# Last powers in bf16, paired table copies, a shorter gate mask and a new written order: a gated attention and state-space mix on one NeuronCore

## The chip, the cores and the metric

The kernel runs on 1 core of a Trainium2 chip. The metric is the device time of one execution in microseconds (us). The program is one launch; nothing is computed on the host. Five engines work side by side: PE (matrix products; its weight loads are shown apart as PEld), ACT (scalar engine), DVE (vector engine), POOL, and SP, which here issues every DMA.

## The reference

An input `x` of 2048 tokens by 512 channels goes through two branches that are mixed by a gate for each token.

```
g = sigmoid((x * gate_w).sum(-1))                 # one gate for each token
a = A(x)        # 32 heads of 16 channels, 4 segments of 512 tokens:
                # causal softmax attention inside a segment, plus a linear
                # memory of the earlier segments (M, z), mixed by sigmoid(beta)
b = B(x)        # diagonal state-space model, 512 channels x 128 states:
                # K[d,l] = Re sum_n C[d,n] dB[d,n] exp(dt A[d,n] l)
                # y = causal convolution of x with K (by FFT), + x * Dskip
out = g * a + (1 - g) * b
```

The positions `l` of the convolution are rounded to bf16 in the reference, so only some of the 2048 exponents differ.

## The kernel before

**Attention.** For each segment `s` and each group `hg` of 8 heads the kernel projects keys and queries (`project`, tags `pk`, `pq`; `ko` is a masked copy of the keys), makes the values (`seg_tokens`, tags `tok`), five score tiles of 128x2048 with an exponential on ACT (`scores`, tags `sc`, L1067), a causal mask product on DVE from the second half of the segments on (`mk`, L1079), products with the values (`pv`), a division (`nrm`, L1041 and L1042), the memory part (`mem`, with feature maps `fq`), a transpose (`oT`), and at the end the output projection (`fin`). There are 80 score tiles; their exponentials are the largest work of ACT.

**Convolution kernel.** `ssm_prep` computes the complex step factor Z for two halves `h` of the channels. `ssm_powers` squares it again and again: power k is Z to 2^k, kept in f32 (a square on ACT, L785; a subtraction and a product on DVE, L786 and L787), copied to bf16 (tag `pwc`, L793 on ACT or L794 on DVE), with a negated half (L795) and a 64 KB DMA that puts the real part in a second place. `tables(c)` then makes, for each of four chunks `c` of 128 channels, two tables F (20 entries) and G (32 entries) of products of powers: four copies of powers into F and one copy of the coefficients into G (tag `tabc`, by the helper `evac`, L226 on ACT or L227 on DVE), twelve complex products of three DVE instructions each (tags `tab<c>.<n>`, L1180, L1183, L1187), then 8 groups of small matrix products (tag `lag<c>`, PE, 128x40) whose results are evacuated by ACT or DVE and sent by DMA into `KTT`.

**Convolution.** `x_level1` transforms x and writes it to a DRAM scratch (`xl1`). `tail(half)` runs 16 steps `t` for each half: it loads constants (`CT`, 192 KB, and `CD`, 320 KB, both c_DNM) and x (`Zx`), makes X and the transformed kernel K on PE, exchanges the halves of X by two 64 KB DMAs, multiplies on DVE (`Y`, L1298), transforms back (`V`), and writes. `fir` and `Cl` finish and bring the result into the token layout for `fin`. K of half a needs lag0 and lag1, K of half b needs lag2 and lag3.

**Order.** The text `ORDER` sets everything: each entry is the number of an operation, with `a` (ACT) or `v` (DVE) where either engine can run it, and the buffer slots that it takes. An engine runs its operations strictly in that order; SP issues its DMAs strictly in that order. `S.replay` reads the text and `S.emit` writes the waits. On one engine the tags stand thus in the order before:

```
DVE  ... tab1.11 tab1.11 nrm0.3.1 pk1.1 sm0.1 ...
SP   ld_prm0 ld_ident ld_prm0 ld_dt xTl0 xl1l0 ld_W1 ld_prm1 ld_small
     ld_prm1 ld_wq0 ld_prm2 ld_negm ld_wk0 ld_mk ld_small ld_prm2 ld_wv ...
SP   ... Xb15 Xb15 CDb2 Xb3 Xa15 CTb5 Xa15 Xb3 CDb3 CTb1 Zxb6 CDb4 ...
```

**Gates.** `gates` makes the mask `gmaskT` (544 columns, f32) in two steps: L865 copies 512 gate values into it, L866 multiplies all 544 columns by the block mask `bdT`.

Of the kernel before, what the change touches and what calls it, by code (L numbers as in the profile page):

```python
# [7 lines left out]
ACT = mybir.ActivationFunctionType  # L8
# [501 lines left out]
def build_graph(nc, es, A_x, A_wq, A_wk, A_wv, A_wo, A_beta, B_A_re, B_A_im, B_B_re, B_B_im,  # L510
# [264 lines left out]
    def ssm_powers(Zs):  # L775
        Zc = list(Zs)
        for k in range(10):
            for h in range(2):
                S.tag = "pow%d.%d" % (h, k)
                Z = Zc[h]  # L780
                pw = Tile(pwP, BF16)
                pws[(k, h)] = pw
                if k < 9:
                    sq, nz = Tile(sqPs[h], F32), Tile(ZPs[h], F32)
# [676 lines left out]
```

## Time and profile before

| | |
|---|---|
| median of 3 runs | 287.18 us (286.94 to 287.20) |
| the profiled execution | 287.07 us, its span 285.3 us |
| PE busy | 248.9 us (87%) |
| DVE busy | 265.6 us (93%), 634 instructions |
| ACT busy | 261.4 us (92%), 314 instructions |
| POOL busy | 5.9 us |
| granted clock of PE | 0.994 on average |

The span runs from the first to the last instruction; 1.8 us of the execution's own time lie around it. A line of a group gives the busy time, the mean duration of one instruction, and the idle time of its engine just before. Durations on DVE and ACT overlap: the next instruction starts before the one ahead has ended, so what a piece of work costs its engine is the distance from start to start. Times in the timeline are from the start of the span.

### The profile page before, as it was taken

What the parts mean: (1) busy time and instruction counts of PE and PEld (TensorE: products, weight loads), DVE (VectorE), ACT (ScalarE), POOL (GpSimd) and SP (SyncE); (2) the same over time, 40 slices, a digit from 0 to 9 for tenths busy, and PEclk for the clock granted to TensorE, in tenths of its full rate; (3) what the DMA queues carried; (4) which work ended last, traced back from release to release, by engine and by line L of the source; (5) the groups of instructions that cost most, each with busy time, mean ns of one, the idle gap of its engine ahead of it and who ended that gap; (6) DMA issues with size and microseconds to landing.
All of it is one profiled execution on the core that took longest, in us unless ns stands there. A gap on an engine that the chain in (4) does not pass through costs nothing.

```text
span 285.3 us, 9041 instructions
## 1 busy us (share of the span) xinstructions
PE 248.9 (87%) x3741; PEld 170.4 (60%) x3776; DVE 265.6 (93%) x634; ACT 261.4 (92%) x314; POOL 5.9 (2%) x9
## 2 busy tenths in 40 slices
PE   2767778788687999999999899999989999999995
PEld 1423444465344756777767477876766676889552
DVE  1999999999999999999999999996889999999795
ACT  2999999999999999989999999999878999998832
POOL 0003100000001000000001000000000000000000
PEclk9999997999999999999999999999999999999999
DMA  6969364402825727653656576787667876356966
GB/s 179 212 209 169 97 155 149 149 7 84 122 88 169 181 58 208 186 165 87 177 174 194 137 219 181 194 242 200 192 199 210 258 209 190 77 146 175 264 175 203
DMA packets 61211, 47.71 MB, mean 167 GB/s; under 512 B 23921, under 2 KB 57074, under 8 KB 61170
## 3 DMA queue, kind: packets, MB, share of 16 engines
q1 hardware_dynamic: 61170, 47.13, 60.1%
q8 instruction: 30, 0.49, 0.8%
q14 instruction: 11, 0.09, 0.1%
HBM read 26.79 MB, written 8.39 MB: 123 GB/s over the span
## 4 chain that ended last, share of the span: by engine, by line
PE 35%; DVE 33%; ACT 26%; issue 2%; DMA 2%; SPq 0%; DVEq 0%
PE psum L663 34%; ACT sb L1067 16%; ACT sb L226 8%; DVE sb L1180 5%; DVE sb L1187 5%; DVE sb L1183 5%; DVE sb L227 3%; DVE sb L794 2%; DVE sb L787 2%; DVE sb L786 2%; DMA sb<-sb 1%; DVE sb L1042 1%; DMA sb<-in_B_A_im_dram 1%; ACT sb L940 1%; DVE sb L795 1%
## 5 line engine op out<-in xcount | busy, mean ns | idle before, releaser
L663 PE MATMUL psum<-sb 128*128 128x17 bf16 (+12 forms) x3605 | 241.3, 231 | 26.8 <-ACT sb L1067 14.3
L663 PEld LDWEIGHTS psum<-sb 128*128 128x128 bf16 (+4 forms) x3640 | 161.3, 99 | 100.9 <-ACT sb L1067 27.5
L1067 ACT ACTIVATE sb<-psum 128x2048 bf16<-128x2048 f32 x80 | 152.1, 1901 | 4.7 <-PE psum L663 3.8
L226 ACT ACTIVATE sb<-psum 128x512 bf16<-128x512 f32 (+4 forms) x154 | 88.4, 628 | 3.2 <-PE psum L663 2.8
L1180 DVE TENSOR_TENSOR sb<-sb 128x512 bf16<-128x512 bf16 (+3 forms) x48 | 33.0, 697 | 0.0
L1187 DVE TENSOR_TENSOR sb<-sb 128x512 bf16<-128x512 bf16 (+3 forms) x48 | 32.1, 681 | 0.0
L1183 DVE TENSOR_TENSOR sb<-sb 128x512 bf16<-128x512 bf16 (+3 forms) x48 | 31.9, 674 | 0.0
L227 DVE CAST sb<-psum 128x512 bf16<-128x512 f32 (+2 forms) x41 | 27.6, 674 | 3.0 <-PE psum L663 2.8
L1079 DVE TENSOR_TENSOR sb<-sb 128x1024 bf16<-128x1024 bf16 (+1 forms) x40 | 22.4, 569 | 1.3 <-ACT sb L1067 1.2
L1298 DVE TENSOR_TENSOR sb<-sb 128x1024 bf16<-128x1024 bf16 x32 | 21.7, 680 | 1.9 <-DMA sb<-sb 1.8
L1042 DVE TENSOR_TENSOR sb<-psum,sb 128x256 bf16<-128x256 f32 x32 | 13.2, 414 | 0.1
L227 DVE COPY sb<-psum 128x512 bf16<-128x512 bf16 (+2 forms) x15 | 7.2, 480 | 5.7 <-PE psum L730 5.3
L785 ACT ACTIVATE sb<-sb 128x512 f32<-128x512 f32 x18 | 11.8, 656 | 0.0
L1368 ACT ACTIVATE sb<-psum,sb 128x512 bf16<-128x512 f32 x8 | 5.2, 689 | 5.7 <-DMA out_dram<-sb 5.5
L1041 DVE RECIPROCAL sb<-psum 128x16 f32<-128x16 f32 x32 | 7.9, 248 | 1.4 <-PE psum L663 1.3
L912 POOL COPY sb<-sb 128x128 bf16<-128x128 bf16 x4 | 5.5, 1462 | 149.1 <-PE psum L663 124.0
L1121 DVE TENSOR_TENSOR sb<-psum,sb 128x512 bf16<-128x512 f32 x12 | 8.2, 684 | 0.1
L794 DVE CAST sb<-sb 128x512 bf16<-128x512 f32 x19 | 8.0, 434 | 0.0
L996 ACT ACTIVATE sb<-sb 128x512 bf16<-128x512 bf16 x12 | 7.5, 636 | 0.1
L940 ACT ACTIVATE sb<-psum 128x512 bf16<-128x512 bf16 x12 | 7.6, 637 | 0.0
L1337 DVE TENSOR_TENSOR sb<-psum,sb 128x512 bf16<-128x512 f32 x11 | 7.4, 687 | 0.2 <-PE psum L663 0.2
L786 DVE TENSOR_TENSOR sb<-sb 128x256 f32<-128x256 f32 x18 | 7.5, 417 | 0.0
(74 smaller groups left out, 120.7 us busy)
## 6 DMA issues: line engine op xcount, KB each, us to landing
sb<-c_DNM SPq DMA_DIRECT2D x28, 320.0 KB, 3.8
sb<-sb SPq DMA_DIRECT2D x84, 64.0 KB, 2.9
sb<-c_DNM SPq DMA_DIRECT2D x28, 192.0 KB, 3.1
scr_Z<-sb SPq DMA_DIRECT2D x16, 256.0 KB, 2.2
sb<-scr_Z SPq DMA_DIRECT2D x32, 128.0 KB, 3.1
sb<-sb SPq DMA_DIRECT2D x32, 128.0 KB
sb<-in_A_x_dram SPq DMA_DIRECT2D x5, 512.0 KB, 4.8
scr_C<-sb SPq DMA_DIRECT2D x8, 256.0 KB, 2.6
```

The lines of the kernel that those rows point to most:

```text
L226: fa = lambda e: e.activation(dst(), src(), ACT.Copy)
L227: fd = lambda e: e.tensor_copy(dst(), src())
L663: mm = lambda e, o_, l, r_, st, sp, **kw: e.matmul(o_, lhsT=l, rhs=r_, start=st, stop=sp, skip_group_check=True, **kw)
L786: op("DVE", ("V1", 256), lambda e, nz=nz, sq=sq: e.tensor_tensor(ap(nz, 0, n=256), ap(sq, 0, n=256), ap(sq, 256, n=256), ALU.subtract), r= ...
L794: "DVE": (("Vs2", 512), lambda e, dst=dst, src=src: e.tensor_copy(dst(), src()))})
L1042: op("DVE", ("V1", 256), lambda e: e.tensor_tensor(ap(o1, gi * 16, [[128, 4], [32, 4], [1, 16]]), ap(T, dims=[[68, 4], [17, 4], [1, 16]]), ...
L1067: o = op("ACT", ("Ax", 2048), lambda e, P=P, pT=pT: e.activation(ap(pT, n=2048), ap(P, n=2048), ACT.Exp, scale=0.25), r=[P], w=[pT])
L1079: op("DVE", ("V2", 128 * nb), lambda e, pT=pT, dims=dims: e.tensor_tensor(ap(pT, dims=dims + [[1, 128]]), ap(pT, dims=dims + [[1, 128]]), ...
L1180: op("DVE", ("V2" if n > 1 else "V1", 256 * n), lambda e: e.tensor_tensor(run(tile, ne, dst, 1), run(tile, ne, src, sstep), fac(cl * 512), ...
L1183: op("DVE", ("V2" if n > 1 else "V1", 256 * n), lambda e: e.tensor_tensor(run(t2, n, 0, 1), run(tile, ne, src, sstep), fac(cl * 512 + 256) ...
L1187: op("DVE", ("V2" if n > 1 else "V1", 256 * n), lambda e: e.tensor_tensor(D_(), D_(), ap(t2, n * 128, [[-n * 128, 2], [2 * n, 64], [1, 2 * ...
L1298: op("DVE", ("V2", 1024), lambda e, Y=Y, XAB=XAB, K3=K3: e.tensor_tensor(ap(Y, dims=[[512, 2], [1, 512]]), ap(XAB, dims=[[512, 2], [1, 512 ...
```

## The change

1. **Powers** (`ssm_powers`). At k = 8 the square of power 8 is written straight into the bf16 tile of power 9 (subtraction and product with bf16 outputs). The f32 tile for it and its copy are gone, once for each half: two copies fewer.
2. **Tables** (`tables`). Four copies of 256 columns into F become two of 512 columns: entries 2 and 3 (powers 1 and 2), entries 4 and 11 (powers 3 and 0). Eight copies fewer in all; the copy into G stays.
3. **Gate mask** (`gates`). The 512 gate values are multiplied by the block mask on their way into `gmaskT`; the other 32 columns get a product of their own.
4. **Order.** A new text `ORDER`. Operations from power 9 on have new numbers.

```diff
@@ ssm_powers
                 if k < 9:
+                    pws[(k, h)] = Tile(pwP, BF16)
+                pw = pws[(k, h)]
+                if k == 8:
+                    last = Tile(pwP, BF16)
+                    pws[(9, h)] = last
+                    sq = Tile(sqPs[h], F32)
+                    half = lambda T, o: ap(T, o, [[128, 2], [1, 128]])
+                    op("ACT", ("As", 512), ... ACT.Square ...)
+                    op("DVE", ("V1", 256), ... e.tensor_tensor(ap(last, 0, [[512, 2], [1, 128]]), half(sq, 0), half(sq, 256), ALU.subtract) ...)
+                    op("DVE", ("V1", 256), ... e.scalar_tensor_tensor(ap(last, 256, [[512, 2], [1, 128]]), half(Z, 0), 2.0, half(Z, 256), ALU.mult, ALU.mult) ...)
+                elif k < 9:
...
-                op("ANY", 0, None, r=[Z], pw=[pw], ... copy to bf16, ACT or DVE ...)
+                if k < 9:
+                    op("ANY", 0, None, r=[Z], pw=[pw], ... copy to bf16, ACT or DVE ...)
@@ gates
-        op("DVE", ("V1", 512), lambda e: e.tensor_copy(ap(gmaskT, dims=[[17, 32], [1, 16]]), ap(growT, dims=[[1, 32], [0, 16]])), r=[growT], w=[gmaskT])
-        op("DVE", ("V1", 544), lambda e: e.tensor_tensor(ap(gmaskT, dims=[[136, 4], [1, 136]]), ... ap(bdT, dims=[[0, 4], [1, 136]]), ALU.mult), r=[bdT], w=[gmaskT])
+        op("DVE", ("V1", 32), lambda e: e.tensor_tensor(ap(gmaskT, 16, [[136, 4], [17, 8]]), ... ap(bdT, 16, [[0, 4], [17, 8]]), ALU.mult), r=[bdT], w=[gmaskT])
+        op("DVE", ("V1", 512), lambda e: e.tensor_tensor(ap(gmaskT, 0, [[136, 4], [17, 8], [1, 16]]), ap(bdT, 0, [[0, 4], [17, 8], [1, 16]]),
+                                                         ap(growT, 0, [[8, 4], [1, 8], [0, 16]]), ALU.mult), r=[bdT, growT], pw=[gmaskT])
@@ tables
-        for e_, k_ in ((11, 0), (2, 1), (3, 2), (4, 3)):
-            S.evac(lambda e_=e_: ap(F, 2 * e_, [[FPL, 2], [2 * NF, 64], [1, 2]]),
-                   lambda k_=k_: ap(pws[(k_, h)], cl * 512, [[256, 2], [2, 64], [1, 2]]), 256, ...)
+        for e0, e1, ka, kb in ((2, 3, 1, 2), (4, 11, 3, 0)):
+            def src2(ka=ka, kb=kb):
+                a_ = ap(pws[(ka, h)], cl * 512, n=1)
+                return ap(pws[(ka, h)], cl * 512, [[ap(pws[(kb, h)], cl * 512, n=1).offset - a_.offset, 2], [256, 2], [1, 128]])
+            S.evac(lambda e0=e0, e1=e1: ap(F, 2 * e0, [[2 * (e1 - e0), 2], [2 * NF, 128], [1, 2]]), src2, 512, ...)
@@ ORDER (two entries as an example: xT0, then CTb5)
-59a
+59v
-1583/4
+1573/2
```

What the new order changes, read from the text by tags:

- Evacuations that change engine ahead of the lag products of chunk 3: from ACT to DVE one of `xT0` (1024 columns), `pwc1.8`, one of `lag1`, `tok2.0` and `Va9`; from DVE to ACT one of `oT0`. Of the table copies, two of chunk 1 and one of chunk 3 were on ACT; now all eight paired copies are on DVE, and the G copy of chunk 1 is on ACT. Later ones go both ways: 11 from DVE to ACT and 11 from ACT to DVE among X, K and V of the convolution, and a few of `lag3`, `fir`, `oT`, `pk`, `pq` and `gts`.
- DVE ahead of the last product of chunk 3: `diag` (128 columns) and one `fq1.3` newly stand before it, one `sm1.0` no longer does. Ahead of the last product of chunk 0 newly stand three products of the second half's powers 2 and 3; at the end of chunk 1 they stand before it in both orders.
- PE: the operations ahead of each chunk's lag products are the same set in both orders, except one `pv1.0` that moves behind lag1. At the start PE now runs `xl1 xl1 xl1 pk0.0 xl1 prm1 pq0.0 tok0.3 prm2 sc0.0` instead of `xl1 xl1 xl1 prm1 pq0.0 pk0.0 prm2 tok0.1 sc0.0`.
- SP at the start: `ld_prm0 ld_ident ld_prm0 ld_dt xTl0 ld_small ld_W1 xl1l0 ld_wk0 ld_wq0 ld_prm1 ld_wv ld_mk ld_prm1 ld_prm2 ld_negm ld_prm2 ...`: the value weights (`ld_wv`, 512 KB) stand ahead of the second half of the B coefficients (`ld_prm1`) and of both loads of the C coefficients (`ld_prm2`).
- SP at step 5 of half b: `... Xb15 Xb15 Xa15 CTb5 Zxb1 CDb2 Xa15 CDb4 CTb1 Xb3 CDb3 Xb2 ...`: the constants of step 5 (`CTb5`) now go ahead of `CDb2` and of the exchange of step 3.

More of the change, by code (lines that the diff above doesn't have):

```diff
@@ L440 @@
+951/1/1/0 912 952 1770/0/2 934 927/1 953 944/0/3 954 945 1728 1760/2/3 935 931 1742/3/4 913/4 1729 946 1732/5/5 1771 932 914v 1772 1507/0 1761 936
+1765 1773 939/0 1762 943 947 937/0 1766 948 1743 1744 1739/4/2 1767/2/3 1745 1731 1746/3/1 949/4 1737 938/1 950 1733 955 1740 1738 1778/6/4 956/1
+1753/0/0 1734 957a 1741 1779 1768 1780 1769 1774/1/5 1747 1756/2/2 1775 1757 1754 1787/7/3 1788 1748 1781 1755 1776 1749/6/1 1783/4/0 1758 1789 1782
+1790 1777 1759 1791 1750 1751 1752 1784 1785 1786
 """
@@ L780, in ssm_powers @@
                 Z = Zc[h]
-                pw = Tile(pwP, BF16)
-                pws[(k, h)] = pw
                 if k < 9:
+                    pws[(k, h)] = Tile(pwP, BF16)
[5 more added lines that the diff above has]
+                    half = lambda T, o: ap(T, o, [[128, 2], [1, 128]])
+                    op("ACT", ("As", 512), lambda e, sq=sq, Z=Z: e.activation(ap(sq, n=512), ap(Z, n=512), ACT.Square), r=[Z], w=[sq], key=PW[h] + PWS * k)
+                    op("DVE", ("V1", 256), lambda e, last=last, sq=sq, half=half: e.tensor_tensor(ap(last, 0, [[512, 2], [1, 128]]), half(sq, 0), half(sq, 256), ALU.subtract),
+                       r=[sq], pw=[last], key=PW[h] + PWS * k)
+                    op("DVE", ("V1", 256), lambda e, last=last, Z=Z, half=half: e.scalar_tensor_tensor(ap(last, 256, [[512, 2], [1, 128]]), half(Z, 0), 2.0, half(Z, 256), ALU.mult, ALU.mult),
+                       r=[Z], pw=[last], key=PW[h] + PWS * k)
+                elif k < 9:
                     sq, nz = Tile(sqPs[h], F32), Tile(ZPs[h], F32)
@@ L791, in ssm_powers @@
                 dst = lambda pw=pw: ap(pw, 0, [[512, 2], [256, 2], [1, 128]])
-                op("ANY", 0, None, r=[Z], pw=[pw], key=PW[h] + PWS * k + 0.3, alts={
-                    "ACT": (("As", 512), lambda e, dst=dst, src=src: e.activation(dst(), src(), ACT.Copy)),
-                    "DVE": (("Vs2", 512), lambda e, dst=dst, src=src: e.tensor_copy(dst(), src()))})
+                if k < 9:
+                    op("ANY", 0, None, r=[Z], pw=[pw], key=PW[h] + PWS * k + 0.3, alts={
+                        "ACT": (("As", 512), lambda e, dst=dst, src=src: e.activation(dst(), src(), ACT.Copy)),
+                        "DVE": (("Vs2", 512), lambda e, dst=dst, src=src: e.tensor_copy(dst(), src()))})
                 op("DVE", ("V4", 256), lambda e, pw=pw: e.tensor_scalar(
```

144 lines of the change are left out of this document (70 added, 74 removed).

## Prediction

> **What bounds the kernel now.** I read three views: the busy time of the engines by stage, the chain of waits where a stage ends, and the timeline of DVE there. I cut the stages where the lag products of chunks 1, 2 and 3 start, at about 92.4, 128.0 and 165.3 us.
>
> ```profile
> core 0: us, PE busy (x) PEld busy (x) DVE busy (x) ACT busy (x) POOL busy (x), PEclk, DMA share, GB/s
> 6.40:92.40 86.00, 65.54 (x903) 37.56 (x915) 85.82 (x214) 84.90 (x113) 4.73 (x3) 0.98 0.55 135
> 92.40:128.00 35.60, 33.52 (x575) 24.36 (x580) 35.49 (x85) 33.73 (x43) 0.00 (x0) 1.00 0.58 162
> 128.00:165.30 37.30, 34.68 (x553) 24.61 (x558) 36.83 (x82) 37.21 (x48) 0.73 (x1) 1.00 0.55 155
> 165.30:280.60 115.30, 111.89 (x1700) 82.38 (x1713) 104.31 (x251) 103.02 (x112) 0.00 (x0) 1.00 0.69 197
> ```
>
> Up to 165 us DVE is idle for 0.18, 0.11 and 0.47 us in the three stages; ACT is nearly as full, PE has room. From 165 us on PE is the full one: 111.89 of 115.30. So ahead of lag3 work on DVE counts, behind it only what keeps PE waiting. The joint between the two is the last table product of each chunk, on which the lag products wait:
>
> ```profile
> 91.95 0.31 DVE sb L1187
> 92.25 0.14 issue
> 92.39 3.50 PE psum L663 x156
> ...
> 126.34 1.49 DVE L1187 TENSOR_TENSOR sb<-sb 128x512 bf16<-128x512 bf16 x2
> ...
> 129.27 0.45 ACT L226 ACTIVATE sb<-psum 128x320 bf16<-128x320 f32 x1
> ...
> 159.11 0.69 DVE L1298 TENSOR_TENSOR sb<-sb 128x1024 bf16<-128x1024 bf16 x1 [0.36 <-DMA sb<-sb]
> ...
> 162.99 1.56 DVE L1187 TENSOR_TENSOR sb<-sb 128x2048 bf16<-128x2048 bf16 x2
> ...
> 164.11 0.39 PE psum L663 x2
> ...
> 164.55 4.60 PE psum L663 x163
> ...
> 166.79 0.58 ACT L226 ACTIVATE sb<-psum 128x480 bf16<-128x480 f32 x1
> ```
>
> At chunk 1 DVE ends at 92.25 and PE starts 0.14 later, straight from the chain. At chunk 2 DVE ends at 127.83 and the first evacuation follows 1.44 later. At chunk 3 DVE ends at 164.55 and the first evacuation by ACT comes 2.24 later. PE there still had a projection of four products to run behind the piece at 164.11, so chunk 3 has a slack of at most 2.24 - 1.44 = 0.8 us; chunks 1 and 2 have none to speak of.
>
> **The change part by part.** On DVE I count starts, not durations. These rows give the distances:
>
> ```profile
> 18.18 0.42 DVE L794 CAST sb<-sb 128x512 bf16<-128x512 f32 x1
> 18.51 0.69 DVE L809 TENSOR_TENSOR sb<-sb 128x512 f32<-128x512 bf16 x1
> 19.12 0.42 DVE L794 CAST sb<-sb 128x512 bf16<-128x512 f32 x1
> ...
> 23.81 0.69 DVE L227 CAST sb<-psum 128x512 bf16<-128x512 f32 x1
> 24.41 0.41 DVE L767 TENSOR_TENSOR sb<-sb 128x256 f32<-128x256 f32 x1
> ...
> 30.68 0.69 DVE L227 COPY sb<-sb 128x256 bf16<-128x256 bf16 x4
> 31.22 0.21 DVE L795 TENSOR_SCALAR sb<-sb 128x256 bf16<-128x256 bf16 x1
> ...
> 118.72 0.29 DVE L998 TENSOR_SCALAR sb<-sb 128x512 bf16<-128x512 bf16 x1
> 118.92 0.18 DVE L1118 TENSOR_SCALAR sb<-psum 128x32 f32<-128x32 f32 x1
> ...
> L866 DVE TENSOR_TENSOR sb<-sb 128x544 f32<-128x544 f32 x1 | 0.7, 662 | 0.0
> ...
> L865 DVE COPY sb<-sb 128x512 f32<-128x512 f32 x1 | 0.4, 420 | 0.0
> ...
> L226 ACT ACTIVATE sb<-sb 128x256 bf16<-128x256 bf16 x3 | 1.5, 486 | 0.0
> ...
> L940 ACT ACTIVATE sb<-psum 128x512 bf16<-128x512 bf16 x12 | 7.6, 637 | 0.0
> ```
>
> A cast of a power costs DVE 0.33, an f32 product of 512 columns 0.61, an evacuation from PSUM 0.60, a table copy of 256 columns 0.54/4 = 0.135, and a bf16 pass of 512 columns 0.20.
>
> *Powers.* Both copies that go were on DVE: -2 x 0.33 = -0.67. The bf16 outputs I cost at nothing: the product of 256 f32 columns (0.33) has the same length in f32, and the nearest row, the cast, writes bf16 at no less a rate.
>
> *Table copies.* DVE had 17 of the 20, 17 x 0.135 = 2.30. It now has eight pairs and three G copies. A pair is a bf16 pass of 512 columns: 8 x 0.20 + 3 x 0.135 = 2.00. Net -0.30. Bounds of a pair: two separate copies (0.27) and the f32 rate (0.33); I take 0.20, the row of the same type and size. The Trainium skill ("VectorE: DVE Perf Modes", "The DRAIN you can't avoid") says that the next instruction does not start before the pipe is empty. By that each copy would cost its full 0.29 us, the pairs would save 1.7 us, and DVE would be up to 1.4 us earlier at chunk 3 than below; the four copies in 0.54 us say no.
>
> *Gate mask.* Out go L866 (about 0.58 by starts) and L865 (0.33), in come 0.61 and a pass of 32 columns, 0.18 long as the one at 118.92 and some 0.1 by starts: -0.2.
>
> *Order, on DVE ahead of the last product of chunk 3.* Newly on DVE: one `xT0` 0.60, `pwc1.8` 0.33, one `lag1` 0.58, `tok2.0` 0.60, `Va9` 0.60, `diag` 0.16, `fq1.3` 0.20: +3.07, each by the distances above at its number of columns. Gone or later: one `oT0` 0.33, `sm1.0` 0.35: -0.68. All of it: -0.67 - 0.30 - 0.23 + 3.07 - 0.68 = **+1.2 us** of DVE work. At chunk 1 the same count gives -0.2, at chunk 2 +0.2; at chunk 0 it gives +1.1, since three products of the second half's powers (0.33 each) stand ahead there; they are due anyway by chunk 1, so PE and ACT wait there and get it back.
>
> *Order, on ACT.* Ahead of lag3 ACT loses `xT0`, `pwc1.8`, `lag1`, `tok2.0`, `Va9` (0.64 of duration for 512 columns, the first about 1.0) and three table copies (0.49), and gains an `oT0` and a G copy: -3.9 in durations, about -3 by starts. I cost this gain at nothing: what hides it is DVE, and PE goes no earlier than the tables. If DVE is not the limit, it comes out (first rival).
>
> *At lag3.* DVE ends 1.2 later, less its one wait in this stretch (0.36 for a DMA at 159.11, which may or may not recur), less the slack of 0.8: between +0.04 and +1.2. By the pieces at 164.11 and 164.55 PE had two products and a projection (4 x 0.27 by the group row below) to go, so most of the slack was there: I take **+0.45**.
>
> ```profile
> L663 PE MATMUL psum<-sb 128*128 128x512 bf16 x253 | 67.9, 391 | 7.2 <-DVE sb L1042 1.6 <-DVE sb L227 1.4 <-DVE sb L941 1.1
> ```
>
> *Start.* SP puts the 512 KB of `ld_wv` ahead of the second `ld_prm1`, so 2.46 MB stand up to it instead of 1.67 MB. What rate do these rows allow?
>
> ```profile
> 5.28 0.69 DVE L227 COPY sb<-psum 128x1024 bf16<-128x1024 bf16 x1 [5.28 <-PE psum L730]
> ...
> GB/s 179 212 209 169 97 155 149 149 7 84 122 88 169 181 58 208 186 165 87 177 174 194 137 219 181 194 242 200 192 199 210 258 209 190 77 146 175 264 175 203
> ...
> sb<-in_A_wv_dram SPq DMA_DIRECT2D x1, 512.0 KB, 5.0
> ...
> 11.23 1.06 PE L730 MATMUL psum<-sb 128*128 128x128 bf16 x8
> ...
> 12.17 2.76 PE L663 MATMUL psum<-sb 128*128 128x512 bf16 x8
> ```
>
> The first two slices of 7.13 us carry 1.28 and 1.51 MB, so 2.46 MB have moved by 12.7 us and are seen some 1 to 2 us later: 13.5 to 14.5. Then PE runs `prm1` (1.06), `pq0.0` and `tok0.3` (eight products, 2.76), and DVE can evacuate `tok0.3` at 17.3 to 18.3. By its own work it comes there at 17.7 (its 35 instructions ahead come to 11.3 us by starts, from 5.28 on, and it waits about 1.1 us among its first two). So DVE stands still for 0 to 0.6; I take **+0.3**, and since DVE is never idle afterwards this goes through to lag3. The Trainium skill ("DMA: Bandwidth & Descriptors", "Queues, rings and completion order") says that an engine takes its descriptors in ring order, which speaks against this edit: the late load then carries the whole of `ld_wv`.
>
> *Behind lag3.* PE has the same products to do; DVE and ACT have about as much (-0.2 and -0.1). So a shift at lag3 goes to the end, but for PE's one long wait in there:
>
> ```profile
> 206.88 0.61 DVE sb L1079
> 207.50 0.65 issue
> ...
> 208.14 4.03 PE L663 MATMUL psum<-sb 128*128 128x256 bf16 x56 [1.26 <-DVE sb L1079]
> ...
> 202.76 0.58 SPq L222 DMA_DIRECT2D sb<-c_DNM  x1
> ...
> sb<-c_DNM SPq DMA_DIRECT2D x1, 192.0 KB, 5.3
> ...
> sb<-c_DNM SPq DMA_DIRECT2D x28, 192.0 KB, 3.1
> ```
>
> The product that starts late at 208.14 is `Xb5`. Its constants `CTb5` are the DMA issued at 202.76, and with 5.3 us to landing they are there at 208.05; the median of such loads is 3.1. The new order issues `CTb5` ahead of `Zxb1` and `CDb2` (128 and 320 KB), two issues of about 0.5 us earlier. If it lands by 206.9 the whole 1.26 us close; if the mask product that ends at 207.49 was a true condition, 0.65 close. I take **-1.05**, nearer to the upper end, as one DVE pass of `fq3.0` also leaves the way of that mask product. SP moves that I cost at nothing: the third transposing load of x gives place to the first, and the 64 KB exchanges of the powers go behind it; the first table product is no earlier than before, so their cover is as it was.
>
> *Sum* against the profiled execution's own 287.07: +0.45 + 0.3 - 1.05 = -0.3, so **286.8 us**. That execution is 0.11 below the median of 287.18; I let this stand.
>
> **The rivals.**
>
> *First, faster, 285.3 us: DVE is not the limit between lag2 and lag3, ACT is.* For it: ACT is busy 37.21 of these 37.30 us, DVE 36.83, and there ACT loses `tok2.0`, `Va9` and a table copy (0.5 + 0.5 + 0.3) and gains an `fq2.0` (0.5). Against it: DVE was as full in the two stages before, and a DVE that waits for nothing can't be overtaken. It would give -0.8 at lag3 in place of +0.45, no stop at the start, and the -1.05: 285.2 to 285.4. A small part of it (2 in 100 of all) is the page's empty pipe from above, by which DVE would gain 1.4 us and the end be near 285.5.
>
> *Second, slower, 288.1 us: the second B coefficients land late.* The place is the start: PE runs strictly in order, so `prm1` holds back `pq0.0`, `tok0.3` and `prm2`, and DVE stands at `tok0.3`. For it: the value load took 5.0 us in the trace of before, and the third slice carries more traffic still. Against it: the rate of the first two slices. From a landing at about 14.9 on, it decides; one at 15.5 makes the stop 1.6 instead of 0.3, and the end 286.8 + 1.3 = 288.1, with DVE never idle later to take it up.
>
> *Third, no change in place of a gain: the copies in pairs don't run at the rate of the bf16 pass.* At 0.33 each, eight of them cost 1.0 more, of which the slack takes some: 287.3. The row with 0.20 has one run of 512 columns, the pair writes two columns at a time; but so do the four copies at 0.135.
>
> **How the numbers follow.** A difference of 0.2% (0.57 us) is about what a measurement of this kernel can tell from no change; below, faster means under 286.6, slower over 287.75. My forecast, 286.8 with its own bounds 286.2 to 287.5 (lag3 +0.04 to +1.2, start 0 to 0.6, tail -1.26 to -0.65, not all at one end), gets 0.38, of which 0.10 lie under 286.6. The first rival gets 0.30, all faster; the second 0.27, all slower; the third 0.05, no change. So faster 0.40, same 0.28 + 0.05 = 0.33, slower 0.27. The range 285.1 to 288.6 leaves out about a tenth on either side: of the first rival what lies beyond a full -1.26 and -0.8, of the second a landing past 16.
>
> **What would show it.** In the profile of the changed kernel: DVE copies of 128x512 bf16 from SBUF to SBUF, eight, of some 0.29 us each, with starts 0.20 apart where two stand together; no cast at L794's place beyond eighteen; DVE ending its last table product of chunk 3 at 165.4 to 166.0 and the first evacuation of lag3 about 1.4 to 1.6 later, where ACT now waits for PE; a DVE wait of 0.3 ahead of its first evacuation from PSUM of 512 f32 columns; no PE wait over 0.3 us at `Xb5`. It makes the prediction wrong if DVE has new waits between 20 and 150 us, where it had none, if DVE ends chunk 3 before 165, or if another load takes the place of `CTb5` in the tail.

## The result, and the profile after

The changed kernel takes 289.18 us (median; 288.32 to 290.39), the kernel before 286.94 us on the same chip: a ratio of 1.009, 95% interval 1.0068 to 1.0111 (the ratios here are estimated from all the single executions and need not be the quotient of the two medians). One execution of the changed kernel, 303.59 us at a granted clock of 0.845, is left out of the range and the ratio. The changed kernel is slower by 2.2 us, where 0.3 less was forecast. The profiled execution of the changed kernel took 288.32 us with a span of 286.5, that of the kernel before 287.07 and 285.3; so the profile holds 1.25 of the 2.2 us. The profiled execution was the shortest of the ten that are left; a second profile (E9, 289.12 with a median of 289.29) lies near its median and is read beside it below.

The stages, cut where the lag products of chunks 1 to 3 start (now 92.5, 128.7 and 166.2):

```profile
core 0: us, PE busy (x) PEld busy (x) DVE busy (x) ACT busy (x) POOL busy (x), PEclk, DMA share, GB/s
6.40:92.50 86.10, 64.16 (x898) 36.97 (x899) 85.73 (x211) 83.25 (x109) 5.83 (x3) 1.00 0.52 131
92.50:128.70 36.20, 34.49 (x598) 24.88 (x600) 36.10 (x86) 34.73 (x43) 0.00 (x0) 1.00 0.56 162
128.70:166.20 37.50, 35.15 (x557) 24.64 (x557) 37.39 (x82) 36.16 (x44) 2.82 (x1) 1.00 0.56 162
166.20:283.30 117.10, 114.98 (x1720) 82.45 (x1719) 105.89 (x252) 103.66 (x112) 0.00 (x0) 1.00 0.69 198
```

DVE is as full as before, ACT has more room ahead of lag3 than it had, and the last stretch is 117.10 us long where it was 116.99 before (165.29 to the end of TensorE, PE in the views, at 282.29). The start of lag3 is taken from its first product, 165.29 and 166.21 us. Its first weight load comes with it or up to 0.03 us ahead (first block from the kernel before, second from the changed one; TensorE itself does not stand ahead of lag3 in either):

```profile
165.29 1.60 PEld L663 LDWEIGHTS psum<-sb 128*64 128x64 bf16 x96 [0.42 <-ACT sb L226]
```

```profile
164.23 1.55 DVE L1200 TENSOR_TENSOR sb<-sb 128x2048 bf16<-128x2048 bf16 x2
164.98 1.60 PE L663 MATMUL psum<-sb 128*128 128x256 bf16 x19
...
166.18 0.33 PEld L663 LDWEIGHTS psum<-sb 128*64 128x64 bf16 x14 [0.44 <-DVE sb L954]
```

DVE's last table product ends at 165.78 (164.55 before: +1.23), lag3 starts 0.92 later. The difference of the two executions is then lag3 +0.92, the stretch from lag3 to TensorE's end +0.11, and what follows it +0.20 (the last DVE work ends 0.98 behind TensorE, 0.78 before): 1.23 of the 1.25.

In that last stretch the long wait at `Xb5` is gone, yet the stretch is no shorter. The view of TensorE's waits behind lag3, before (waited for: us in total, times, the longest) and after:

```profile
PE psum L663 <- DVE sb L1079: 1.3, 1, 1.3
PE psum L663 <- issue: 0.3, 2, 0.2
PE psum L663 <- ACT sb L1067: 0.2, 1, 0.2
PE psum L663 <- DMA sb<-c_DNM: 0.2, 1, 0.2
PE psum L663 <- DVE sb L227: 0.2, 1, 0.2
```

```profile
PE psum L663 <- ACT sb L1080: 1.4, 4, 0.5
PE psum L663 <- ACT sb L1009: 0.3, 1, 0.3
PE psum L663 <- DVE sb L1134: 0.2, 1, 0.2
```

One wait of 1.3 has gone and four waits for exponentials (L1080; L1067 is the same line before), 1.4 together, stand where one of 0.2 stood. Two of the rows name an engine where it was a load. The 1.3 is put down to a mask, on which `Xb5` does not depend in the program; it starts at 208.14, 0.09 us after `CTb5` has landed (208.05), and in all seven profiles with a wait at `Xb5` (before, E1, E4, E6, E11, E15, E16) it starts 0.09 after that landing. The 0.3 for L1009 is the wait of `Ka14` for its load `CDa14`, which lands at 176.98, 0.13 ahead of the product; `Ka14` does not depend on L1009. The 0.2 for c_DNM in the kernel before is the same wait there.

### The profile page after: what moved, and what is told of

It is laid out like the page before. It is cut to its first block, busy times and chain, and to the rows that moved or that the text cites. A ratio compares the mean times of both kernels' runs of the same rounds, so it can differ in the third digit from the quotient of the medians.

```text
span 286.5 us, 9058 instructions
## 1 busy us (share of the span) xinstructions
PE 250.4 (87%) x3776; PEld 169.8 (59%) x3776; DVE 266.8 (93%) x629; ACT 259.7 (91%) x308; POOL 9.1 (3%) x9
## 4 chain that ended last, share of the span: by engine, by line
PE 35%; ACT 27%; DVE 26%; DMA 5%; issue 4%; SPq 1%; DVEq 0%
PE psum L663 34%; ACT sb L1080 15%; ACT sb L226 8%; DVE sb L1196 4%; DMA sb<-sb 4%; DVE sb L1200 4%; DVE sb L227 4%; DVE sb L1193 4%; DVE sb L1313 2%; ACT sb L796 1%; DVE sb L806 1%; ACT sb L1009 1%; DVE sb L1055 1%; DMA sb<-in_B_A_im_dram 1%; SPq L222 1%
## 5 line engine op out<-in xcount | busy, mean ns | idle before, releaser
L1080 ACT ACTIVATE sb<-psum 128x2048 bf16<-128x2048 f32 x80 | 151.4, 1893 | 5.2 <-PE psum L663 4.1
L226 ACT ACTIVATE sb<-psum 128x512 bf16<-128x512 f32 (+2 forms) x153 | 85.6, 610 | 9.3 <-PE psum L1150 5.0
L227 DVE CAST sb<-psum 128x512 bf16<-128x512 f32 (+2 forms) x43 | 28.7, 673 | 1.7 <-PE psum L663 1.2
L925 POOL COPY sb<-sb 128x128 bf16<-128x128 bf16 x4 | 8.6, 2263 | 153.8 <-PE psum L663 130.3
L227 DVE COPY sb<-psum 128x512 bf16<-128x512 bf16 (+1 forms) x14 | 7.1, 508 | 5.2 <-PE psum L730 5.2
L796 ACT ACTIVATE sb<-sb 128x512 f32<-128x512 f32 x16 | 10.4, 652 | 0.5 <-DVE sb L767 0.5
L1134 DVE TENSOR_TENSOR sb<-psum,sb 128x512 bf16<-128x512 f32 x12 | 8.2, 686 | 0.2
L1352 DVE TENSOR_TENSOR sb<-psum,sb 128x512 bf16<-128x512 f32 x12 | 8.1, 687 | 0.4 <-PE psum L663 0.3
L1009 ACT ACTIVATE sb<-sb 128x512 bf16<-128x512 bf16 x12 | 7.4, 629 | 0.0
L806 DVE CAST sb<-sb 128x512 bf16<-128x512 f32 x18 | 7.3, 418 | 0.0
L1380 DVE SCALAR_TENSOR_TENSOR sb<-psum,sb 128x512 bf16<-128x512 f32 x8 | 5.8, 745 | 1.3 <-DMA out_dram<-sb 1.3
```

What stands on the lines that cost most here:

```text
L226: fa = lambda e: e.activation(dst(), src(), ACT.Copy)
L227: fd = lambda e: e.tensor_copy(dst(), src())
L796: op("ACT", ("As", 512), lambda e, sq=sq, Z=Z: e.activation(ap(sq, n=512), ap(Z, n=512), ACT.Square), r=[Z], w=[sq], key=PW[h] + PWS * k)
L1009: op("ACT", ("Asx", 512), lambda e: e.activation(ap(eq, n=512), ap(qT, n=512), ACT.Exp), r=[qT], w=[eq])
L1080: o = op("ACT", ("Ax", 2048), lambda e, P=P, pT=pT: e.activation(ap(pT, n=2048), ap(P, n=2048), ACT.Exp, scale=0.25), r=[P], w=[pT])
```

## The experiments

"Edits" are the three edits to powers, copies and gate; "old order" and "new order" the texts before and after. lag3 and TensorE's end are of the one profiled execution, and "the stretch" is the time between the two.

| | kernel | its time / before, us | ratio, 95% interval | lag3 starts | lag3 to end of TensorE |
|---|---|---|---|---|---|
| | before | 286.94 | | 165.29 | 116.99 |
| E15 | before, second profile | 287.61 (one run) | | 165.46 | 117.37 |
| | changed | 289.18 / 286.94 | 1.009, 1.0068 to 1.0111 | 166.21 | 117.10 |
| E9 | changed, again | 289.29 / 287.19 | 1.0089, 1.0054 to 1.0125 | 166.56 | 117.46 |
| E1 | edits, old order | 287.22 / 286.53 | 1.003, 0.9997 to 1.0063 | 165.14 | 116.25 |
| E16 | the same, again | 287.32 / 287.17 | 1.0018, 0.9981 to 1.0056 | 165.26 | 116.66 |
| E2 | new order without the edits | 291.84 / 286.53 | 1.0178, 1.0139 to 1.0217 | 168.63 | 116.72 |
| E3 | old order to lag3, new behind | 288.71 / 286.53 | 1.0068, 1.0043 to 1.0092 | 165.34 | 118.13 |
| E4 | new order to lag3, old behind | 292.71 / 286.53 | 1.0193, 1.0145 to 1.0241 | 167.07 | 120.67 |
| E5 | E1, CTb5 ahead of Zxb1 | 288.77 / 287.37 | 1.0053, 1.0024 to 1.0083 | 165.50 | 118.50 |
| E6 | changed, CTb5 late | 292.72 / 287.37 | 1.0186, 1.0143 to 1.0229 | 168.21 | 118.17 |
| E7 | changed, old final sequence | 292.67 / 287.37 | 1.0168, 1.0124 to 1.0212 | 167.86 | 120.19 |
| E8 | changed, four evacuations back on ACT | 291.22 / 287.37 | 1.0124, 1.0082 to 1.0165 | 167.19 | 117.17 |
| E10 | changed, Xa5 exchanges together | 290.22 / 287.19 | 1.01, 1.0067 to 1.0134 | 166.81 | 117.42 |
| E11 | E1, tok2.0 on DVE | 286.94 / 287.19 | 0.9998, 0.9976 to 1.0021 | 166.78 | 116.59 |
| E12 | changed, last scores later | 291.62 / 287.19 | 1.0145, 1.0108 to 1.0181 | 166.49 | 118.51 |
| E13 | changed, xT0 back on ACT | 290.38 / 286.94 | 1.011, 1.0075 to 1.0146 | 168.73 | 117.95 |
| E14 | changed, CDa14 ahead of CDa13 | 289.05 / 286.94 | 1.0076, 1.0048 to 1.0103 | 166.93 | 116.43 |
| E17 | E11, CTb5 behind CDb2, fq3.0 later | 286.75 / 287.17 | 0.9987, 0.9955 to 1.0018 | 165.44 | 115.54 |

**E1 and E16, the edits alone; E2, the order alone.** The edits were put into the order of before (or taken out of the new one), each operation at its old place and slot.

```
E1, E16: code of the changed kernel; ORDER of before, renumbered:
         -casts of power 9 (x2), -copies 3 and 4 of each four into F; the rest at its old place and slot
E2:      code of before; ORDER of the changed kernel, renumbered:
         +casts of power 9 (x2), each where the power is used next, +copies 3 and 4 of F behind copies 1 and 2
```

> The three edits alone (last powers, pair copies, gate mask) in the order of before. Theory 1 (the loss is made by the new order, the edits alone save 1.2 us of DVE work ahead of the last table product of chunk 3): that product ends 0.4 to 1.2 us earlier than 164.55 and the time is 0.2 to 1.2 us under before, near 286.2. Rival A (an edit itself costs: the pair copies or the bf16 outputs are slow, or make others wait): 287.8 to 289.2, and the chunk-3 product ends no earlier than in before.

> The new order alone, with the powers, copies and gate mask of before. Theory 1: the time is at or over that of the changed kernel, 289.2 to 290.4, since the order makes the loss and the 1.2 us that the edits save on DVE are missing; the last table product of chunk 3 ends at 166.2 to 167.0 (165.78 in the changed kernel). Rival A: 286 to 287.5, as the loss goes with the edits.

> The three edits alone in the order of before, a second time. Theory 4 (what they take off DVE becomes a wait of DVE, since ScalarE is as full): DVE's waits up to the end of the chunk-3 tables are 0.6 to 1.4 us more than the 6.45 to 6.72 of the kernel before, its last table product ends 0 to 0.4 us earlier than 164.55, the time is within 0.5 us of the kernel before. Rival (they are worth their 1.27 us): the product ends near 163.4 and the time is 0.8 to 1.2 us less.

Counted by starts up to the end of the chunk-3 tables, E1's DVE does 1.27 us less than before: the casts of the powers -0.68, the table copies -0.34, the gate -0.25. But its last table product ends only 0.25 earlier (0.08 in E16), because DVE now waits where it did not: 7.22 us in all up to there in E1 and 7.70 in E16, for 6.45 and 6.72 in the two profiles of before (5.2 to 5.5 of each is the wait for the first load). DVE's waits from 6.4 to 165 us, before and in E1:

```profile
DVE sb L752 <- ACT sb L741: 0.5, 1, 0.5
DVE sb L1298 <- DMA sb<-sb: 0.4, 1, 0.4
```

```profile
DVE sb L1313 <- DMA sb<-sb: 0.7, 1, 0.7
DVE sb L752 <- ACT sb L741: 0.5, 1, 0.5
DVE sb L227 <- PE psum L663: 0.3, 1, 0.3
DVE sb L1193 <- DMA sb<-sb: 0.2, 1, 0.2
```

No difference from before can be measured in either run. E2 is the other half: without the edits the new order costs 1.0178, with them 1.009, so inside the new order the edits are worth some 2.6 us (291.84 to 289.18), and DVE's last table product ends at 168.20 (166.65 and 1.55) where it ends at 165.78 with them. Rival A is out in both, though E2 goes beyond theory 1 too (at most 290.4, and 167.0 for that product), and E1 stays short of it; what was expected of E16 came. What an edit on DVE is worth depends on who is the limit, and the chain of waits says who. Its shares between 130 and 164.5 us, before, in E1 and after:

```profile
by line: ACT sb L1067 54.0%; ACT sb L226 35.6%; issue 4.4%; PE psum L663 3.9%; ACT sb L996 1.5%; ACT sb L940 1.4%
```

```profile
by line: ACT sb L1080 53.6%; ACT sb L226 36.4%; PE psum L663 4.5%; issue 3.2%; ACT sb L1009 1.5%; ACT sb L953 1.4%
```

```profile
by line: ACT sb L1080 25.9%; PE psum L663 16.3%; ACT sb L226 14.9%; DVE sb L1193 7.8%; issue 7.4%; DVE sb L227 5.9%; DVE sb L1196 4.6%; DVE sb L1200 3.5%; DVE sb L1313 3.5%; ACT sb L1009 3.3%; DVE sb L1134 2.0%; DVE sb L1000 1.8%; DVE sb L9
```

Before, nine tenths of this chain are ACT, its exponentials and evacuations, and no DVE line is in it. In the new order the chain goes to and fro between ACT, TensorE and DVE. Up to the tables of chunk 1 it is otherwise: there the chain of the kernel before runs on DVE, and what the edits save comes out, for in E1 those tables end 0.49 us earlier (91.75 for 92.24) with no more waiting than before (5.85 and 5.89). What they save behind that is what turns into waits. The chain of the kernel before from 60 to 92.3 us:

```profile
by line: DVE sb L1180 22.8%; DVE sb L1187 22.1%; DVE sb L1183 21.2%; DVE sb L227 7.8%; DVE sb L794 6.2%; DVE sb L787 4.4%; DVE sb L786 4.1%; DVE sb L1042 3.1%; DVE sb L795 2.3%; DVE sb L1041 2.1%; issue 1.8%; DVE sb L987 1.4%; DVE sb L941 1
```

**E3 and E4, heads and tails exchanged.**

```
E3: first 1033 entries of the old order, then the rest as in the new one
E4: first 1030 entries of the new order, then the rest as in the old one
```

> The edits, the order of before up to the first lag product of chunk 3, and the new order behind it (with the earlier load of CTb5 and the new sequence at the end). Theory 1a (the shift at lag3 and the new sequence of the final products share the loss, the earlier CTb5 gives 1.3 back): lag3 starts 1.2 to 1.9 us earlier than in the changed kernel, and the time is 287.2 to 288.2. Theory 1b (the loss is all in the head: start and DVE load): 285.0 to 286.2. Theory 1c (the loss is all behind lag3): 288.7 to 289.3.

> The edits, the new order up to the first lag product of chunk 3, and the order of before behind it (late CTb5, old sequence at the end). Theory 1a: lag3 as late as in the changed kernel, the product behind CTb5 waits again, the end as in before: 287.6 to 288.6. Theory 1b (loss in the head): 289.0 to 290.5, as the earlier CTb5 is lost too. Theory 1c (loss behind lag3): 286.2 to 287.2.

Both miss. E3 has the lag3 of the old order (165.34), but a wait of 0.96 at 177 us, and E4 one of 1.43 at 173, which neither order has by itself; probably the two orders do not fit each other at the joint. So the times of these two say little about head or tail. Two things remain. The head alone sets lag3. And the waits behind lag3 come with the order behind lag3: E3 has the four waits for exponentials of the changed kernel, each of the same length (0.20, 0.32, 0.40 and 0.48), and the wait at `Ka14` (0.6), E4 the one of before (0.2). E2 has the four as well, so the edits do not make them. The rows of E3, then of E4:

```profile
PE psum L663 <- ACT sb L1080: 1.4, 4, 0.5
PE psum L663 <- DMA sb<-c_DNM: 0.6, 1, 0.6
```

```profile
PE psum L663 <- ACT sb L1080: 0.2, 1, 0.2
```

**E5, E6 and E17, the load of CTb5.**

```
E5:  SP (old order)  ... Vb12 +CTb5 Zxb1 Xb15 Xb15 CDb2 Xb3 Xa15 -CTb5 Xa15 ...
E6:  SP (new order)  ... Xa15 -CTb5 Zxb1 CDb2 +CTb5 Xa15 ...
E17: SP (old order)  ... Xb15 Xb15 CDb2 +CTb5 Xb3 Xa15 -CTb5 Xa15 ...; tok2.0 a -> v; fq3.0 behind mk2.2.B1
```

> The three edits in the order of before, with one load moved: CTb5 is issued right ahead of Zxb1, as in the new order. Theory 2 (TensorE is full behind lag3; closing the gap at Xb5 lets it run ahead of ScalarE, so part of the gain comes back as waits for exponentials): the gap of 0.755 us at 207.25 (edits in the old order) goes, TensorE ends 0.75 earlier than 281.39 less new waits on exponentials of 0.3 to 0.75, time 0 to 0.5 us under the edits in the old order. Theory 1 (the gap is simply gone): no new waits on exponentials over 0.15, TensorE ends at 280.5 to 280.8, time 0.6 to 0.9 us under the edits in the old order.

> The changed kernel with one load moved back: CTb5 is issued behind the first Xa15 load, as before the change. Theory 1: the wait at Xb5 is back with 0.7 to 1.3 us and goes to the end: the profiled TensorE end moves from 283.31 to 284.0 to 284.6, time 0.7 to 1.3 over the changed kernel. Theory 2: the wait at Xb5 is back, but the later waits on exponentials (0.40 at 231.7, 0.48 at 269.5) shrink by as much as they are made by it: TensorE end within 0.5 of 283.31.

> The edits in the order of before, with tok2.0 on DVE, CTb5 issued right behind CDb2 (where its buffer is free, so that SP does not stand), and the pass fq3.0 behind the mask product that Xb5 waits for. Expected: CTb5 lands near 206, the wait at Xb5 (0.65 to 0.76) falls to 0.2 to 0.45, the stretch from lag3 to the end of TensorE is 115.8 to 116.2 in place of 116.25 to 116.6, time 0.2 to 0.8 us under the kernel before. Rival (the wait at Xb5 moves to Yb15 or to the next exchange, as when CTb5 was issued ahead of Zxb1): time 0.3 to 1.5 over.

E5 closes the wait at `Xb5` and opens longer ones, which neither theory expected. The queue rows of SP say why (us of start, length):

```profile
198.74 0.66 SPq L222 DMA_DIRECT2D sb<-sb  x1
201.77 0.32 SPq L222 DMA_DIRECT2D sb<-c_DNM  x1
202.14 0.43 SPq L222 DMA_DIRECT2D sb<-scr_Z  x1
202.93 1.15 SPq L222 DMA_DIRECT2D sb<-sb  x2
```

```profile
207.37 0.69 DVE L1313 TENSOR_TENSOR sb<-sb 128x1024 bf16<-128x1024 bf16 x1 [1.88 <-DMA sb<-sb]
```

SP stands from 199.40 to 201.77 in front of `CTb5`, whose buffer is still in use, and the exchange of `Xb15` stands behind it; DVE waits 1.88 us for that exchange at `Yb15`, and TensorE 1.42 for DVE. The load was early, the queue was late. E6 gives the wait at `Xb5` back, with the 1.29 us of the row below, and the stretch grows to 118.17 (117.10 and 117.46 in the two profiles of the changed kernel); the waits for exponentials stay as they were (0.20, 0.32, 0.40, 0.48), so they are not made by TensorE running ahead, and theory 2 is out.

```profile
211.27 1.38 PE L663 MATMUL psum<-sb 128*128 128x256 bf16 x12 [1.29 <-DVE sb L1092]
```

E6's median is 3.5 us over that of the changed kernel, where 0.7 to 1.3 was expected; in its profile 2.0 stood already at lag3, at an order that is the same up to there (some 0.8 to 0.9 of it from the stretch of low clock in the last part, 0.74 a wait of DVE at `Ya5`). E17 issues `CTb5` four places later than E5, behind both exchanges of `Xb15` and `CDb2`, where its buffer is free: it lands at 204.82, TensorE has no wait at `Xb5`, and the stretch is 115.54, the shortest of all.

```profile
PE psum L663 <- DVE sb L227: 0.4, 2, 0.3
PE psum L663 <- ACT sb L1080: 0.2, 1, 0.2
PE psum L663 <- issue: 0.2, 1, 0.2
```

Against E1 and E16 that is 0.71 and 1.12 less, with `fq3.0` moved as well as the load. E17 is the version that the experiments pointed to; its profiled execution took 285.79 us. Its ratio to the kernel before, 0.9987, has an interval that holds 1: no gain can be claimed, but it is faster than the changed kernel.

**E7 and E12, the end.**

```
E7:  PE from 262 us on: products, transposes and final products in the old sequence (old PE, ACT, DVE places)
E12: PE  ... fin2.3 pv3.3.A0 -sc3.3.B1 fin2.0 pv3.3.B0 +sc3.3.B1 fin0.3 ...
```

> The changed kernel with the sequence of before among the last value products, output transposes and final products (from about 262 us on). Theory 1a (the three final products that the new order puts behind oT3.3 make the loss at the end): last DVE work 1.0 to 1.7 us earlier than 284.29, time 1.0 to 1.7 under the changed kernel. Theory 2 (TensorE is full up to its end, and what it does last makes no difference): TensorE ends within 0.4 us of 283.31, time within 0.5 of the changed kernel.

> The changed kernel with the last block of scores (sc3.3.B1) behind the next two products on TensorE (fin2.0, pv3.3.B0), as before the change. Theory 5 (the waits of TensorE for exponentials, new behind lag3, come from scores placed ahead of the exponential that frees their bank): the wait of 0.48 us at 269.5 goes, TensorE ends 0.3 to 0.5 earlier against its lag3 start (117.1 to 116.6 to 116.8), time 0.3 to 0.5 under the changed kernel. Rival: the last exponential comes later and the value products wait for it instead; 0 to 0.3 over.

Both are slower. E7 has new waits of TensorE of 1.55, 0.91 and 0.77 us at 270, 279 and 283: the old sequence does not fit what the new order has done by then. Theory 1a gets no support from it, but with these waits it is no clean test of it either. In E12 the wait of 0.48 is gone, and 0.35 and 1.01 have come in its place, the second for the exponential that now comes later: this is what its rival said, but the time is 2.3 over E9's, not 0 to 0.3. Its profile also has the longest wait of all at `Ka14`, 1.27.

**E8, E11 and E13, work between ACT and DVE.**

```
E8:  tok2.0, Va9, lag1 (third), pwc1.8 (cast)   v -> a   (new order)
E13: xT0 (first)                                v -> a   (new order)
E11: tok2.0                                     a -> v   (old order, edits)
```

> The changed kernel with four evacuations given back to ScalarE (tok2.0, Va9, one of lag1, one cast of power 8), in the same places of the order. They are 2.05 us of DVE by starts. If DVE sets lag3 alone: DVE ends the tables of chunk 3 at 163.7 in place of 165.78, lag3 starts 1 to 2 us earlier than 166.21 and the time falls by that. If ScalarE is the next limit right behind: DVE gets waits of 1 to 1.5 us, lag3 starts at 165.1 to 165.7, time 0.4 to 1.0 under the changed kernel.

> The changed kernel with the first evacuation xT0 given back to ScalarE, where ScalarE idles 1.1 us more than before ahead of the tables of chunk 0. By the DVE count (DVE is full from the start and 0.60 us lighter): the last table product of chunk 0 ends 0.4 to 0.7 us earlier than in the changed kernel of the same chip (59.16), lag3 starts at 165.9 to 166.2 in place of 166.56, time 0.3 to 0.6 under the changed kernel (289.3). Rival (ScalarE is the limit as well): lag3 within 0.2 of 166.56 or later, time no better.

> The three edits in the order of before, and one evacuation (tok2.0, near 139.5 us) on DVE instead of ScalarE. Theory 4 (in the order of before ScalarE is as full as DVE, so what the edits take off DVE turns into a wait of DVE at Ya6; it is worth something only if ScalarE gets lighter too): DVE's wait of 0.71 at Ya6 shrinks to 0.1 to 0.3, its last table product of chunk 3 ends as before (164.2 to 164.6), the exponentials behind 141 us come 0.4 to 0.5 earlier, lag3's first evacuation at 166.1 to 166.3 in place of 166.63, time 0.2 to 0.5 under the edits in the old order. Rival (DVE is the limit after all): DVE ends 0.5 later and the time is 0.3 to 0.6 over.

Giving work back to ACT in the new order buys nothing. In E8 DVE does 1.2 us less up to the end of the tables by starts (2.05 was expected), yet ends them at 165.47 in place of 165.78, for its waits are 1.0 more, 0.73 of it at 105.6 for ACT; lag3 is later, at 167.19. In E13 DVE waits for ACT at the very start:

```profile
DVE sb L767 <- ACT sb L765: 0.8, 1, 0.8
DVE sb L751 <- ACT sb L741: 0.5, 1, 0.5
DVE sb L954 <- ACT sb L953: 0.4, 1, 0.4
DVE sb L1313 <- DMA sb<-sb: 0.4, 1, 0.4
DVE sb L768 <- ACT sb L762: 0.4, 1, 0.4
```

So taking back these moves does not mend the head: DVE, given less, waits for ACT. (E13's profile is the slowest of its six executions, with the granted clock down to 0.50 at 48 and at 58 us, so its lag3 of 168.73 is no measure of the move.) E11's wait of DVE at `Ya6` is gone as expected, but its profiled execution was 1.2 late at lag1 already (93.14, E1 91.90; its granted clock was down to 0.50 at 46 and at 70 us), so its stages tell nothing more; its time is that of the kernel before.

**E9, E10, E14 and E15, typical executions and loads.**

```
E10: SP  ... CTa6 Xa5 -CDa8 Xa5 +CDa8 CDa7 ...
E14: SP  ... CDa12 -CDa13 +CDa14 CTa13 lag3 -CDa14 +CDa13 CTb2 ...
```

> The changed kernel itself, unchanged, for a second profile. Theory 3 (its profile so far, 288.32, was a lucky execution: usually the issue of CTa6 on SP's queue takes 1.0 to 1.5 us instead of 0.49, the second exchange of Xa5 then lands behind the 320 KB of CDa8, and DVE waits 0.4 to 1.4 us at Ya5, near 138 us): the new profile shows such a wait at Ya5, lag3 starts at 167.0 to 168.2 in place of 166.21, and the time is 289.0 to 291. Rival (the profile was typical, the medians differ by the chip alone): no wait over 0.2 at Ya5, lag3 at 166.1 to 166.6.

> The changed kernel with one load moved: CDa8 (320 KB) is issued behind the second exchange of Xa5 instead of between the two. Theory 3: no wait over 0.2 at Ya5, the last table product of chunk 3 ends 0.4 to 1.2 us earlier than in the unchanged kernel of the same call, and the median falls by 0.4 to 1.0. Rival: DVE meets its next wait right behind (at Ya6 or Ya9) and the time stays within 0.3.

> The changed kernel with two loads of 320 KB exchanged on SP's queue: CDa14, which TensorE needs first, is issued ahead of CTa13 and CDa13. Theory 6 (another load has taken the place of CTb5): the wait of 0.3 to 0.6 us at 178 goes, the stretch from lag3 to the end of TensorE falls from 117.46 to 116.8 to 117.1, time 0.3 to 0.6 under the changed kernel. Rival (the wait moves on to CTa13 or to Ka13): a wait of 0.3 or more on a load of constants between 178 and 186, time within 0.3 of the changed kernel.

> The kernel before, unchanged, for a second profile. If its first profile was typical: lag3 starts at 165.1 to 165.5, lag3 to the end of TensorE takes 116.3 to 117.0, with a wait of 0.7 to 1.3 at Xb5. If it was a slow one (its clock was 0.994): lag3 at 164.6 to 165.1, and the distance to the changed kernel is larger than the 0.92 at lag3 that the first two profiles show.

E9 shows no wait at `Ya5`, and E10 no gain (290.22 against 289.29): theory 3 is out as the reason for the distance, though the wait does come in some executions (0.74 in E6, 1.00 in E7). E9 has, behind lag3, a longer wait for a load of constants than the first profile showed:

```profile
176.32 1.13 PE L663 MATMUL psum<-sb 128*128 128x256 bf16 x12
178.06 1.17 PE L663 MATMUL psum<-sb 128*128 128x256 bf16 x9 [0.60 <-DMA sb<-c_DNM]
```

It is `Ka14`, whose `CDa14` lands at 177.93; SP issues it behind `CDa13`, which is needed later, where the order before has it ahead. In the ten profiles with this order of the two loads the wait is 0.30 to 1.27. E14 exchanges the two, and TensorE's waits behind lag3 are one row:

```profile
PE psum L663 <- ACT sb L1080: 1.4, 4, 0.5
```

The stretch falls to 116.43, 0.67 and 1.03 under the two profiles of the changed kernel, as theory 6 expected and a little more. (The Trainium skill, "DMA: Bandwidth & Descriptors", "Queues, rings and completion order", says that an engine consumes descriptors in ring order, though a later one may finish first; in E14 `CDa14`, issued 1.6 us ahead of `CDa13`, lands at 174.70 and `CDa13` at 178.00.) Its median, on another chip, is 0.24 under E9's, too little to tell, so the 0.3 to 0.6 that were expected of the time are not shown. E15, the second profile of before, has lag3 at 165.46 and a wait of only 0.65 at `Xb5`; its stretch, 117.37, is longer all the same, by about 1 us that TensorE's waits do not account for. It is lost behind 262 us, where DVE waits 1.41 us for a load (0.61 in the first profile); whether that is the reason is not shown.

With two profiles of each kernel the distance can be taken in four ways (0.7 to 2.05 us). Between those that lie nearest to their medians it is best covered: E9 (289.12 of 289.29) and the first of before (287.07 of 287.18) give +1.27 at lag3, +0.47 in the stretch behind it and +0.29 in the evacuations behind TensorE's end (1.07 and 0.78), 2.03 of 2.05 us, and the medians of one chip are 2.1 to 2.2 apart. Of the +1.27 some 0.2 is no work of the new order: DVE's very first instruction starts 0.24 later in E9 than in the first profile of the changed kernel, with no instruction changed (the two of before differ by 0.26 in the same way).

## Why the prediction was wrong, step by step

**The sum of DVE work was right, partly by luck.** For the whole change +1.2 was forecast ahead of the last product of chunk 3; by starts it is +1.3, and the product ends 1.23 later. Two of the terms were off and cancelled. The powers were to save 0.67 and the gate 0.23, and saved 0.67 and 0.27. The copies were to save 0.30, but cost 0.16: the eight pairs and three G copies take 2.42 by starts in the changed kernel, for 2.00 in the sum. (In E1, where two pairs are on ACT, they save the 0.34 above, a count that the sum did not make.) The moves of the order were to cost 2.39 net and cost 2.10; the largest part is the `lag1` evacuation, which has 320 columns and takes 0.40, not 0.58. At chunk 0 the last product ends 1.04 later (forecast +1.1), at chunk 1 0.10 (-0.2), at chunk 2 0.59 (+0.2). A pair copy takes 0.42, not 0.29, and the next instruction starts 0.23 to 0.27 later, not 0.20:

```profile
28.44 0.42 DVE L227 COPY sb<-sb 128x512 bf16<-128x512 bf16 x1
28.67 0.47 DVE L825 TENSOR_TENSOR sb<-sb 128x256 bf16<-128x256 f32 x1
```

So the third rival (0.33) is out, and the rule of the empty pipe fails here too. (The Trainium skill itself limits it: "VectorE: DVE Perf Modes", "Two Vector instructions with no wait between them", holds an instruction back when its tensors start in another quarter of the partitions than the last one's. These two use all 128 partitions, so they start in the same quarter, and the trace agrees: the second starts before the first has ended.)

**"So ahead of lag3 work on DVE counts" was a wrong reading behind chunk 1.** Up to 92 us it fits (E1). From there on ACT was just as full (37.21 of 37.30), and the chain from 130 to 164.5 us is ACT's. The chain was read for the joints only, not over the stages. Before, TensorE came to lag3 by way of ACT, and DVE's tables were 0.74 early; in the changed kernel an exponential lets TensorE go on at 164.65, 1.56 us of products stand between it and lag3, and DVE's tables are 0.43 early still. So lag3's shift (0.45 + 0.3 forecast; 0.92 and 1.27 measured) has nearly the right size, but not the path that the prediction gave it: TensorE's own way to lag3 became longer, and DVE did not set it directly. Of the 0.3 at the start nothing came at the place that was named: the second B coefficients landed at 13.73, as forecast, and DVE came to `tok0.3` at 17.84 without a wait; only its waits among its first instructions grew by 0.08 (0.47 and 0.55).

**The 3 us estimated for ACT cost nothing and gave nothing**, as said: its waits up to the end of the tables grew from 6.76 to 8.81. The first rival (285.3) therefore fails in the new order, although in the old one ACT is the limit behind chunk 1. The second rival named the right sign with the wrong place: the load at the start did not hold DVE.

**The step that failed is the term of -1.05 behind lag3: "So a shift at lag3 goes to the end, but for PE's one long wait".** The wait of 1.26 at `Xb5` did close, and it was a wait for that load (E6 brings it back with 1.29; E17, where `fq3.0` moved too, gains 0.7 to 1.1), so the term had the right cause. But the stretch was to be 1.05 shorter and is 0.11 to 0.47 longer than in the first profile of before (against E15 it is 0.27 shorter to 0.09 longer). What failed is that the sum put every other wait of TensorE behind lag3 at no change, though the whole order there was new. The four waits for exponentials are 1.4 together, for 0.2 before, and E3 and E4 show that they come with this order: +1.2, which no term and no rival had. The wait for `CDa14` is 0.3 and 0.6, for 0.2 before, and E14 takes it away; this smaller part is the case named as one that would make the prediction wrong, "if another load takes the place of `CTb5` in the tail". That TensorE has the same products to do was right: less its waits for another engine or a load (1.90, 1.85 and 2.22) the stretch is 115.1 us before and 115.2 in both profiles of the changed kernel. Of the 2.32 us from 286.8 to E9's 289.12, this term is 1.52 (-1.05 to +0.47), lag3 0.52 (0.75 to 1.27) and the evacuations behind TensorE's end, which were costed at nothing, 0.29. With the first profile (288.32) they are 1.16, 0.17 and 0.20. The term was also sized from one execution: the wait is 1.26 in the first profile of before and 0.65 in the second.

What stays open: the waits for exponentials were not resolved one by one, for E12 moved one and made another. No run shows which entries of the new head make lag3 late, only that it is the head's order (E3, E4), that the edits do not do it (E1, E16) and that undoing single moves (E8, E10, E13) did not help. That DVE has 1.3 us more to do and waits nowhere over 0.15 us from 7 us to the end of the tables explains why its tables are 1.23 later, but how that reaches TensorE was not traced.

## What to carry to other kernels

Ask the chain of waits, stage by stage, which engine it runs on before pricing work on the engine that looks full: of two engines with 99% each, lightening one bought nothing that could be measured (E1, E16), and shifting one evacuation between them to even them out did not either (E11). When a whole order is replaced, price the waits of every operation that gets a new place on the full engine, not only the one gap that closes. When the view blames a wait on an engine that had been done for some time, look at the landing of the load (`Xb5`, `Ka14`). A load can only move up on its queue to where its buffer is free (E5 against E17). A difference under 1 us in one stage needs a second profile of both kernels.

## What the runs showed of the hardware

- Kernels with the same instructions in the same order up to lag3 start it, in one profiled execution each, between 166.21 and 168.21 us (the changed kernel, E6, E7, E9, E12, E14).
- The granted clock falls to half for some us in the middle of a kernel whose TensorE never stands long. In E6's profile it does at 42 us (rows of E6, then of the changed kernel; the columns are those of the stages above):

```profile
42.00:44.00 2.00, 2.00 (x35) 1.25 (x37) 2.00 (x5) 2.00 (x3) 0.00 (x0) 0.50 0.57 168
44.00:46.00 2.00, 2.00 (x33) 1.24 (x29) 1.31 (x3) 1.04 (x2) 0.00 (x0) 0.71 0.32 106
```

```profile
42.00:44.00 2.00, 1.75 (x42) 1.28 (x41) 2.00 (x5) 2.00 (x3) 0.00 (x0) 1.00 0.57 168
44.00:46.00 2.00, 0.95 (x24) 0.72 (x21) 2.00 (x4) 1.95 (x2) 0.00 (x0) 1.00 0.46 147
```

TensorE is busy throughout in E6, DVE and ACT run dry behind it. They were 0.24 and 0.23 later than in the changed kernel's profile ahead of it, and are 1.0 and 1.14 later from 45.7 us on, until 60 us at least:

```profile
45.72 0.26 DVE L1054 RECIPROCAL sb<-psum 128x16 f32<-128x16 f32 x1 [0.69 <-PE psum L663]
```

In the profile of before the clock is at 0.50 from 46 to 48 us, and DVE is busy for 2.00 of those 2.00 us: what such a stretch costs depends on the order around it. (The Trainium skill, "TensorE: Matmul & The Clock Gate", "What's actually happening", has two states of the clock, half and full, and a fall to half after an idle window of some 3.4 us. The 0.50 agrees; a stand of that length does not show, as no wait of TensorE's between 20 and 62 us of E6 is over 1.58.)

- These stretches do not make the difference between the kernels. Medians by granted clock, of 19 executions of the changed kernel on two chips and 95 of the kernel before (in brackets, how many have that clock): 289.02 (5) against 286.75 (49) at 1.000, 290.30 (8) against 288.93 (5) under 0.99. They are more frequent in the new order (under 0.995 in 57 of 79 executions of kernels with its head, in 24 of 67 with the old head and the edits, in 30 of 95 of the kernel before), and that adds to its medians; the reason was not looked for.
- One issue on SP's queue can take 1.0 to 1.6 us where it mostly takes 0.5: that of `CTa6` took 0.49 in the changed kernel's profile, 1.48 in E6 and 1.55 in E7, and the exchange behind it was late by as much.
